# Two small additions to the leading products of ones in an attention-and-GLU kernel

## The chip, the core and the metric

The kernel runs on one core of one Trainium2 chip. The metric is the device time of one execution in microseconds (us); the figure given is the median of several runs. A profiled execution has a span, from its first to its last instruction, and a device time of its own, which is a little longer than the span.

## The reference

Two blocks follow each other. The first is a linear attention with a polynomial sketch: with batch 4, 4 heads, 1088 positions and head width 32, each q and k row is multiplied by S1 and S2 (8 x 32), and the outer product of the two results gives 64 features.

```
a = S1 @ x ;  b = S2 @ x ;  phi(x) = outer(a, b)          # 64 features
kv  = sum over s of phi(k)[f] * v[d]      z = sum over s of phi(k)[f]
num = phi(q) . kv                         den = phi(q) . z + 1e-6
attn = num / den                          # (batch, head, seq, 32)
x   = attn, heads side by side            # 4352 tokens x 128
out = (sigmoid(x @ w_gate) * (x @ w_val)) @ w_out        # d_ff = 1536
```

S1, S2 and the three weights reach the program as 64-bit floating-point numbers, seen as pairs of 32-bit words, and are narrowed to 32-bit floats on the chip. All products are of 32-bit floats; a product of a tile pair stands in the trace as two passes of TensorE.

## The kernel before, in words

**The steady part.** The tokens are cut into nine chunks of 512 (the last of 256), and d_ff into twelve blocks of 128. `w1` (L363) makes one "wave": x @ w_gate and x @ w_val for one chunk and one block, four passes of 512 columns. ScalarE takes the sigmoid (L371), VectorE multiplies (L384), and `w2` (L320, `moeout`) adds the product with w_out into a bank. `slot(group, waves)` puts a piece of attention work for the next batch between waves. This part runs from about 19 us to the end.

**The head.** Before the first wave, the attention of the first 512 tokens of batch 0 has to be made, in an order written out by hand; the engines run their own instruction streams in program order. Its steps are:

1. `warm(512, 512)` (call L265, products L261): products of a tile of ones by itself, whose results nobody reads. They need nothing but a memset, and so begin at 0.96 us. The tile they write is one of the two `wave` buffers.
2. S arrives by DMA and is narrowed (`narrow`: L97, L101, L105, L109, L117, L118, L127, on three engines). TensorE turns it (L803, `st`), and VectorE makes the masked copy `sk` (L813).
3. `kps` (L451): k times S for batch 0. VectorE transposes the result (L461, `kab`) and forms features of k in `outer` (L530), for the first five of nine blocks of positions.
4. `aps`, `bps` (L558): q times S, for two pairs of heads. ScalarE copies aps (L568); VectorE multiplies them to the features of q (L577, `qp`). In between stand `gram` (L474, L497), which gives the sum of k's features from small products, its copy (L483), and the mask (L508, L520), whose result `zb` is the denominator's weights.
5. `dps` (L730): the denominator. `kv0` (L638): the product of k's features and v, in two groups: the first five blocks, and the other four after VectorE has made their features. ScalarE copies the result (L674, `kvd`), TensorE turns it (L708, `ndps`), ScalarE copies that (L721, `nd`).
6. `nps` (L749): the numerator; VectorE divides it (L776) into `xT`, the input of the waves, in two halves of 256 tokens.
7. `warm(256)` (L261 again) between nps and the first wave. The first wave is cut into passes of 256 columns, so that it can begin with the first half of xT.

The first weights are narrowed in the same stretch: VectorE has their steps (L105, L109, L127) among those of the attention, POOL has L97 and L118, and ScalarE L101 and L117. All inputs come over the SP and ScalarE DMA queues, the last of the weights at about 23 us.

`warm` builds its operands from `ones` by access patterns that repeat one element:

```
def warm(*cols):
    t = psm.tile([P, 2, 512], F32, tag="wave", name="warm")
    one = [... [0, n] ... for n in cols]      # moving operand, n columns
    x = ... [0, P] ...                        # 128 x 128, stationary
    for r in one: nc.tensor.matmul(out=t[:, 0, :n], lhsT=x, rhs=r, ...)
```

## Time and profile before

| What | Value |
|---|---|
| five runs | 308.75, 309.13, 309.84, 312.97, 313.39 us |
| median | 309.84 us |
| profiled execution, device time | 308.75 us |
| profiled execution, span | 307.0 us |
| TensorE matmul rows busy | 299.2 us (97%) |
| VectorE / ScalarE / POOL busy | 155.3 / 80.8 / 34.4 us |
| waves, L363 | 436 passes, 191.8 us |
| moeout, L320 | 216 passes, 105.5 us |
| warm, L261 | 6 passes, 5.0 us |

A row of the timeline gives the start and the length in us, the engine, the line and operation, the tile written and those read, the shapes and a count; in brackets stands how long the engine had been idle before, and what ended that. Rows on TensorE overlap, since its passes are pipelined: how fast it works is seen from the distance between starts, or from the mean length of one pass of a given shape, and not from the busy share. PEld is its weight load, which can lie beside a pass.

### The profile page before, as it was taken

The page shows a single profiled execution, that of the slowest core. Times are in us where ns is not written, and L with a number is a line of the kernel's source. Part 1 is how long each engine was busy: PE and PEld are TensorE (multiplying, and loading weights), DVE is VectorE, ACT ScalarE, POOL GpSimd, SP SyncE. Part 2 cuts the span into 40 slices and gives each one's busy share as a digit, 9 for nine tenths or more (in the row PEclk, how much of TensorE's full clock was granted, in tenths as well). Part 3 has the DMA queues.
Part 4 walks back from the last instruction along what each step waited for, and adds up shares of the span by engine and source line. Part 5 has one row for each costly group of instructions (what it writes and reads, how often), then busy time and mean ns, then how long its engine had stood idle before and what let it go on. Part 6 is the DMA issues. An engine that isn't in the chain of part 4 may idle for free.

```text
span 307.0 us, 3600 instructions
## 1 busy us (share of the span) xinstructions
PE 299.2 (97%) x1360; PEld 138.2 (45%) x1360; DVE 155.3 (51%) x267; ACT 80.8 (26%) x150; POOL 34.4 (11%) x63
## 2 busy tenths in 40 slices
PE   7889999999999999999999999999999999999994
PEld 2544434444444444533444444444444444444683
DVE  6878889754736544463465542645232223222331
ACT  2356542322122222222123222212222222222220
POOL 1245551230000320000002300000000000000000
PEclk9999999999999999999999999999999999999999
DMA  7992422399402397242003960200001000200011
GB/s 223 320 343 53 124 59 117 81 194 180 153 0 34 78 161 109 61 108 91 0 0 81 184 118 2 35 0 2 0 12 22 0 0 5 31 0 0 7 28 17
DMA packets 29585, 23.29 MB, mean 76 GB/s; under 512 B 20928, under 2 KB 24512, under 8 KB 29568
## 3 DMA queue, kind: packets, MB, share of 16 engines
q1 hardware_dynamic: 25200, 15.21, 18.6%
q0 software_dynamic: 3456, 7.09, 13.4%
q10 hardware_dynamic: 912, 0.77, 0.9%
q8 instruction: 10, 0.16, 0.2%
q14 instruction: 7, 0.06, 0.1%
HBM read 19.80 MB, written 3.26 MB: 75 GB/s over the span
## 4 chain that ended last, share of the span: by engine, by line
PE 96%; DVE 1%; DMA 1%; issue 0%; ACT 0%; SPq 0%; DVEq 0%
PE wave L363 57%; PE moeout L320 30%; PE nps L749 2%; PE dps L730 2%; PE kvz L652 1%; PE kps L451 1%; DMA s_in<-in_S_dram 1%; PE kvz L638 1%; PE cqps L597 1%; PE gram L474 0%; PE bps L558 0%; PE warm L261 0%; PE ndps L708 0%; PE aps L558 0%; DVE kT L428 0%
## 5 line engine op out<-in xcount | busy, mean ns | idle before, releaser
L363 PE MATMUL wave<-xT,w_sb 128*128 128x512 f32 (+1 forms) x436 | 191.8, 566 | 0.0
L384 DVE TENSOR_TENSOR g<-wave,sg 128x512 f32<-128x512 f32 x102 | 70.3, 689 | 130.6 <-ACT sg L371 130.2
L363 PEld LDWEIGHTS wave<-xT,w_sb 128*128 128x128 f32 x436 | 83.2, 191 | 93.0 <-issue 88.5
L371 ACT ACTIVATE sg<-wave 128x512 f32<-128x512 f32 x102 | 60.9, 597 | 201.7 <-PE wave L363 201.7
L320 PE MATMUL moeout<-g,w_sb 128*128 128x512 f32 (+1 forms) x216 | 105.5, 576 | 0.0
L320 PEld LDWEIGHTS moeout<-g,w_sb 128*128 128x128 f32 x216 | 39.5, 190 | 43.6 <-issue 38.5
L621 POOL DMA_DIRECT2D qp<-dq x12 | 7.0, 588 | 110.3 <-DMA dq<-cq 110.3
L118 POOL TENSOR_TENSOR head<-head,tail 128x384 int32<-128x384 int32 (+2 forms) x14 | 13.4, 955 | 20.4 <-DVE head L109 14.2
L530 DVE TENSOR_TENSOR kp<-kab 128x1152 f32<-128x1152 f32 (+2 forms) x10 | 10.8, 1095 | 0.0
L630 DVE TENSOR_TENSOR qp<-qp,bq 128x1152 f32<-128x1152 f32 (+1 forms) x7 | 9.1, 1294 | 2.4 <-DMA bq<-dq 2.4
L109 DVE SCALAR_TENSOR_TENSOR head<-cap,head 128x384 int32<-128x384 int32 (+2 forms) x14 | 7.5, 535 | 0.5
L330 DVE STREAM_TRANSPOSE o_sb<-moeout 128x512 f32<-128x512 f32 (+1 forms) x9 | 6.1, 679 | 2.6 <-PE moeout L320 2.5
L730 PE MATMUL dps<-qp,zb 128*32 128x256 f32 (+1 forms) x64 | 5.8, 434 | 1.4 <-DVE zb L520 1.4
L621 POOL DMA_DIRECT2D bq<-dq x12 | 6.9, 576 | 0.5 <-DMA out_dram<-o_sb 0.2
L127 DVE SCALAR_TENSOR_TENSOR w_sb<-square,head 128x384 f32<-128x384 f32 (+1 forms) x11 | 5.7, 519 | 2.5 <-POOL head L118 2.1
L776 DVE TENSOR_TENSOR xT<-nps,rb 128x576 f32<-128x576 f32 (+2 forms) x9 | 5.9, 660 | 1.9 <-PE nps L749 1.3
L101 ACT ACTIVATE tail<-w_in 128x384 int32<-128x384 uint32 (+1 forms) x13 | 6.6, 522 | 0.9 <-DMA w_in<-in_moe_w_out_dram 0.9
L97 POOL TENSOR_SCALAR cap<-w_in 128x384 f32<-128x384 f32 (+1 forms) x13 | 6.5, 503 | 0.5 <-DMA w_in<-in_moe_w_out_dram 0.5
L749 PE MATMUL nps<-qp,nd 64*32 64x256 f32 (+1 forms) x128 | 6.0, 432 | 0.4 <-ACT nd L721 0.4
L765 DVE STREAM_TRANSPOSE rb<-rc 128x576 f32<-128x576 f32 (+2 forms) x9 | 6.1, 681 | 0.3
L261 PE MATMUL warm<-ones 128*128 128x512 f32 (+1 forms) x6 | 5.0, 972 | 1.0 <-DVE hm L267 1.0
L439 DVE STREAM_TRANSPOSE qT<-kq 128x512 f32<-128x512 f32 (+1 forms) x8 | 5.7, 714 | 0.0
(73 smaller groups left out, 86.9 us busy)
## 6 DMA issues: line engine op xcount, KB each, us to landing
qp<-dq POOLq DMA_DIRECT2D x12, 288.0 KB, 9.2
bq<-dq POOLq DMA_DIRECT2D x12, 288.0 KB, 9.4
v<-in_v_dram SPq DMA_DIRECT2D x16, 144.0 KB, 6.0
kq<-in_k_dram SPq DMA_DIRECT2D x3, 544.0 KB, 3.9
kq<-in_q_dram SPq DMA_DIRECT2D x3, 544.0 KB, 5.2
w_in<-in_moe_w_gate_dram SPq DMA_DIRECT2D x6, 256.0 KB, 5.8
w_in<-in_moe_w_val_dram SPq DMA_DIRECT2D x6, 256.0 KB, 5.5
w_in<-in_moe_w_out_dram SPq DMA_DIRECT2D x6, 256.0 KB, 6.9
```

Source lines behind the costliest of these rows:

```text
L101: nc.scalar.activation(out=tail, in_=lo, func=ACTF.Copy, scale=2.0**-29)
L109: nc.vector.scalar_tensor_tensor(out=head, in0=cap, scalar=-0x40000000, in1=head, op0=ALU.bitwise_and, op1=ALU.bitwise_or)
L118: nc.gpsimd.tensor_tensor(out=head, in0=head, in1=tail, op=ALU.add)
L320: nc.tensor.matmul(out=moe["acc"][:, :tw], lhsT=w_sb[:, 2, j, :], rhs=g[:, jj, :tw], start=(j == 0), stop=(j == NJ - 1),)
L363: nc.tensor.matmul(out=wv[:, which, jj * tw + o : jj * tw + o + tp], lhsT=w_sb[:, which, j0 + jj, :], rhs=xT[:, t0 + o : t0 + o + tp], sta ...
L371: nc.scalar.activation(out=sg, in_=wv[:, 0], func=ACTF.Sigmoid)
L384: nc.vector.tensor_tensor(out=g, in0=wv[:, 1], in1=sg, op=MUL)
L530: nc.vector.tensor_tensor(out=KP[b][:, pi, j0:j1].rearrange("p j m (i l) -> p (j m) i l", i=R), in0=bass.AP(tensor=a0.tensor, offset=a0.of ...
L621: get.dma_start(out=t[64 * c : 64 * c + 64, n * H * W1 : (n + 1) * H * W1], in_=bass.AP(tensor=d0.tensor, offset=d0.offset, ap=rows + [[1, ...
L630: nc.vector.tensor_tensor(out=q0, in0=q0, in1=half(BQ[b], n), op=MUL)
L730: nc.tensor.matmul(out=dps[32 * h : 32 * h + 32, :w], lhsT=zb[b % 2][:, h, :], rhs=half(QP[b], n)[:, 2 * (h % 2) + h // 2, :], start=True, ...
L749: nc.tensor.matmul(out=t[32 * h : 32 * h + 32, c, :w], lhsT=ND[b][rows, 32 * h : 32 * h + 32], rhs=half(QP[b], n)[rows, 2 * (h % 2) + h // ...
```

## The change

The first call of `warm` gets a third product, of 128 columns. A second call, of one product of 128 columns, stands after the turning of S (L803) and before everything that reads its result; on TensorE's stream it comes between `st` and `kps`. Each product is two passes with two weight loads. The second call takes a `wave` buffer of its own, so the later users of that pair of buffers change places. Line numbers after L807 rise by one. TensorE's stream of 398 listed rows has 400; the streams of the other engines hold the same instructions in the same order.

```
-    warm(512, 512)
+    warm(512, 512, 128)
...
     nc.tensor.matmul(out=st_[:, : 2 * R], lhsT=s4..., rhs=ident[...], is_transpose=True, ...)
+    warm(128)
     st_ = st_[:, : 2 * R].rearrange("p (n r) -> p n r", n=2)
     sk = const.tile([P, 2, 2, R], F32, tag="sk")
     nc.vector.tensor_tensor(out=sk, ...)
```

## The prediction

> **What bounds the kernel now.** I read the page first, then TensorE's groups by form in two stretches, then the timelines of TensorE and VectorE up to 20 us. The page shows TensorE on 96% of the chain that ended last.

> ```profile
> span 307.0 us, 3600 instructions
> PE 299.2 (97%) x1360; PEld 138.2 (45%) x1360; DVE 155.3 (51%) x267; ACT 80.8 (26%) x150; POOL 34.4 (11%) x63
> PEclk9999999999999999999999999999999999999999
> PE 96%; DVE 1%; DMA 1%; issue 0%; ACT 0%; SPq 0%; DVEq 0%
> ```

> From 30 us on TensorE stands idle for 3.9 of 277 us. Whatever the head gains or loses before the first wave therefore moves the end by as much, as long as the weights keep up. So the change is worth what it does to the first 23 us.

> The clock row claims full clock throughout, and it is misleading. The same shape takes two lengths. First TensorE's groups by form up to 19.3 us, then from 20 us; the last number before the second bar is the mean length of a pass in ns:

> ```profile
> L451 PE MATMUL kps<-kT,sk 64*32 64x288 f32 x16 | 1.2, 685 | 0.4 <-DVE sk L813 0.4
> L749 PE MATMUL nps<-qp,nd 64*32 64x256 f32 x16 | 1.1, 631 | 0.4 <-ACT nd L721 0.4
> L730 PE MATMUL dps<-qp,zb 128*32 128x256 f32 x8 | 1.1, 631 | 1.4 <-DVE zb L520 1.4
> L363 PE MATMUL wave<-xT,w_sb 128*128 128x256 f32 x1 | 0.6, 634 | 0.0
> L638 PE MATMUL kvz<-kp,v 128*32 128x64 f32 x64 | 2.2, 314 | 0.0
> ```

> ```profile
> L451 PE MATMUL kps<-kT,sk 64*32 64x288 f32 x48 | 2.1, 415 | 0.0
> L749 PE MATMUL nps<-qp,nd 64*32 64x256 f32 x48 | 2.0, 388 | 0.0
> L730 PE MATMUL dps<-qp,zb 128*32 128x256 f32 x24 | 1.9, 391 | 0.0
> L363 PE MATMUL wave<-xT,w_sb 128*128 128x256 f32 x53 | 12.4, 379 | 0.0
> L652 PE MATMUL kvz<-kp,v 128*32 128x64 f32 x192 | 3.3, 220 | 0.0
> ```

> The distances between starts say it plainly: 0.853 us from one 512-column pass of warm to the next, 0.429 in the later waves; 0.427 us for 256 columns at 18.97, 0.216 from 19.97 on. The pass between, from 19.40 to 19.75, took 0.350, so the clock doubled at about 19.67. **TensorE ran at half speed through the whole head**, although 3.41 us of products of ones stand in front of it.

> [...]

> **Part one: 128 more columns at the start.** 128 columns are a quarter of 0.853: 0.213 us a pass, 0.43 for the two, from 4.53 to 4.96; if each waits for its own weight load (0.34 us, the third and fourth of L261), to about 5.1. st waits for `s` until 5.09 and starts at 5.15. Cost at the end: 0 to 0.1 us, hidden by the wait for S. Should S come early, the cost is the whole 0.43.

> **Part two: 128 columns between st and kps.** The gap is in the timeline of TensorE:

> ```profile
> 0.96 3.78 PE L261 MATMUL warm<-ones 128*128 128x512 f32 x4 [0.96 <-DVE hm L267]
> 5.15 0.28 PE L803 MATMUL st<-ident,s 16*128 16x16 f32 x1 [0.41 <-DVE s L127]
> 5.84 1.22 PE L451 MATMUL kps<-kT,sk 64*32 64x288 f32 x16 [0.41 <-DVE sk L813]
> ```

> The nearest row for warm squeezed behind other work is warm(256): its weight load began 0.18 us after nps had streamed, its first pass 0.16 later, and the second weight load took 0.33. Two 128-column passes so placed need about 0.7 us from their first weight load, at 5.4, and let kps go at 6.1 instead of 5.845. Queued behind it are kps and, through it, kab and all of VectorE's head. I take +0.25 for both parts together; the ends are 0 (the passes just fill the gap) and 0.45.

> **What the two buy.** [...] The full clock then comes at 6.01, not 19.67. [...] The head at full speed, step by step:

> - kps starts at 6.1; its second round follows after 0.24, not 0.48, and a row is 0.415 long, not 0.685. kab, at 7.16 before, starts at 6.9.
> - VectorE's kab and kp take 2.29 us as before, to 9.19. Meanwhile aps (1.09 halved), gram (cannot start before kab's first half at 7.3; about 0.8 because of its 36 weight loads) and bps (1.2 halved) end by 8.9. So qp starts at 9.19 and no longer waits for bps. Gain 1.38.

> ```profile
> 7.16 0.85 DVE L461 STREAM_TRANSPOSE kab<-kps 128x288 f32<-128x288 f32 x2 [0.76 <-PE kps L451]
> 10.57 1.29 DVE L577 TENSOR_TENSOR qp<-bps,asb 128x512 f32<-128x512 f32 x2 [1.12 <-PE bps L558]
> 16.43 0.42 DVE L127 SCALAR_TENSOR_TENSOR w_sb<-square,head 128x256 f32<-128x256 f32 x1 [0.33 <-ACT square L117]
> 18.14 0.42 DVE L776 TENSOR_TENSOR xT<-nps,rb 128x256 f32<-128x256 f32 x1 [1.28 <-PE nps L749]
> ```

> - zb and the second half of kp keep that gain: kp ends at 12.06. dps (11.0) and the first group of kv0 end about then. The second group, 1.08 before, takes about 0.6, so kvd starts at 12.8 where it was 15.77. v landed by 9.4.
> - kvd to nps took 1.15; ndps is 0.2 shorter; nps starts at 13.8 and is done by 14.5.
> - VectorE, however, has dT, the reciprocal, rb and five narrowing steps: 13.44 to 16.86 before, 3.4 us with 0.4 of waits. It reaches xT at 15.3, not 18.14: **VectorE takes over the bound**, and the 1.28 us wait for nps goes. Gain 2.85.
> - warm(256) is over by then (it held the first wave from 18.56 to 18.97), and the first eight passes lose their 0.34 of half speed. But the first moeout needs `g` and a narrowed w_out block, which VectorE reached 4.33 us after the first xT; that stays about 4.2. So moeout goes from 22.95 to about 19.9. **Gain 3.0 us**, from there carried to the end.

> The DMAs allow it: w_out's first block landed at 11.2, those of the next pair at 14.0 where their narrowing, at 16.94 before, is wanted at about 14; the later ones have 4 us and more to spare. If that cover failed, the loss is 0.3. The exchanged wave buffers cost nothing: the program's waits on them are the same.

> The sum: 308.75 - 3.0 = 305.75 for a run like the profiled one, span 304.0. The median stands 1.09 above the profiled run. The lowest three runs average 309.24, half a microsecond above it, so I add 0.5: **306.2 us**, 1.2% under 309.84. A measurement of this kernel can tell about 1% from no change, that is 306.74 or less.

> **Rivals.**

> *The clock does not come earlier, or came early in other runs already (0.20).* [...] Against it: none of five runs lies below the late one profiled. Then only the products' +0.25 counts, or the gain is in both kernels: 309.0 to 310.1, say 309.5.

> *The clock comes, but VectorE and the narrowing eat the gain (0.12).* VectorE is over 90% busy from 19 to 26 us. If the weights' chain over three engines shifts by only half of what the attention gains, 1.5 us remain: 307.7. For it: moeout already waited for w_sb in before. Against: POOL and ScalarE have idle time there.

> *The clock comes early and is taken back (0.08), the slower one.* [...] Each us at half clock in the waves costs 0.5. A loss at 16.25 and a return at 19.67 cost 1.7 and leave a gain. The rival decides from a return later than about 22 us; a return at 30 us, (30 - 16.25) / 2 = 6.9 more than 306.2, gives 313.1, which is where the two highest runs of before lie.

> **How the numbers follow.** Forecast 0.60: its own range is 305.0 to 307.4 (kps' delay 0 to 0.45, gain 2.3 to 3.7); about 0.47 falls under 306.74. The rest of it, 0.13, with the first two rivals, 0.32, makes 0.45 within 1%. The slower rival gives 0.08. The range takes in the first rival: 304.9 to 310.2, leaving out the slower one and a few hundredths.

> **What would show it.** Right: the groups by form up to 15 us show kps near 415 ns, dps near 390, kvz near 220; kps starts near 6.1; xT near 15.3; the first wave near 15.7; moeout near 19.9. Part two is wrong if kps starts after 6.4. The forecast falls if kps and nps still take 685 and 631 ns, or if wave passes of 0.853 us appear after 16 us.

## The result and the profile after

The change made no difference that can be measured: the ratio of its executions to those of the kernel before is 0.9983, with a 95% interval of 0.9964 to 1.0002. Medians were 307.57 us (43 executions) and 308.88 us (80). The profiled execution of the changed kernel has a span of 305.7 us and a time of 307.46 us. The comparison leaves out executions more than 1.5% above a kernel's fastest; where I count spans below, I take all but those over 370 us, because the spread itself turned out to be the subject.

First the page of the changed kernel: span, busy times, clock row, chain.

```profile
span 305.7 us, 3608 instructions
PE 298.3 (98%) x1364; PEld 138.5 (45%) x1364; DVE 155.3 (51%) x267; ACT 80.7 (26%) x150; POOL 34.7 (11%) x63
...
PEclk9879999999999999999999999999999999999999
...
PE 96%; DVE 1%; DMA 1%; issue 1%; ACT 0%; SPq 0%; DVEq 0%
```

TensorE is 96% of the chain, as before. The clock row has a dent in its second and third slice, between 7.6 and 22.9 us, where the row of before had none. TensorE's groups by form show what it is. First from 5.6 to 12.3 us, then from 12.4 to 19.1 us:

```profile
L451 PE MATMUL kps<-kT,sk 64*32 64x288 f32 x16 | 0.7, 415 | 0.0
L638 PE MATMUL kvz<-kp,v 128*32 128x64 f32 x32 | 0.7, 221 | 0.2 <-issue 0.2
L730 PE MATMUL dps<-qp,zb 128*32 128x256 f32 x8 | 0.6, 387 | 1.2 <-DVE zb L520 1.2
```

```profile
L363 PE MATMUL wave<-xT,w_sb 128*128 128x256 f32 x6 | 2.6, 614 | 0.0
L749 PE MATMUL nps<-qp,nd 64*32 64x256 f32 x16 | 1.1, 630 | 0.4 <-ACT nd L721 0.4
L638 PE MATMUL kvz<-kp,v 128*32 128x64 f32 x32 | 1.1, 314 | 0.0
```

kps, dps and half of kvz run at full speed (415, 387, 221 ns). The other half of the same kvz takes 314, and nps and the first wave stand where they stood before. **The clock came early, and was taken back in the middle of kv0.** The trace's clock records say when: full speed from 5.53, half from 12.36, full from 19.19 us. The distances between those are 6.83 us each, twice the 3.41 that lie between two changes in the profile of e1_first below (10.85 and 14.26). The view of five stretches of that length, the changes on their edges (columns: stretch, its length, busy us and rows of each engine, granted clock, DMA) shows the stretch before the loss:

```profile
core 0: us, PE busy (x) PEld busy (x) DVE busy (x) ACT busy (x) POOL busy (x), PEclk, DMA share, GB/s
...
5.53:8.95 3.42, 3.32 (x86) 1.63 (x86) 3.16 (x7) 1.52 (x5) 0.54 (x2) 1.00 1.06 239
8.95:12.36 3.41, 1.81 (x50) 1.16 (x50) 3.38 (x9) 1.21 (x4) 1.36 (x4) 1.00 1.08 296
12.36:15.77 3.41, 2.67 (x57) 1.25 (x49) 2.35 (x7) 2.06 (x7) 1.90 (x4) 0.50 1.06 371
15.77:19.19 3.42, 3.42 (x16) 2.74 (x9) 3.14 (x8) 0.69 (x2) 1.29 (x3) 0.50 1.07 375
```

From 8.95 to 12.36 VectorE is busy for 3.38 of 3.41 us and TensorE for 1.81. TensorE waits for VectorE there, 1.18 us of it for zb before dps, and at the end of that stretch the clock is gone. The next two stretches have PEclk 0.50; in the second TensorE is busy for all of its 3.42 us, and at its end the clock is back.

So of the forecast 3.0 us, what is left in this execution is 307.0 - 305.7 = 1.3. The timeline of TensorE in it, and below it three rows of the kernel before:

```profile
5.45 0.51 PE L261 MATMUL warm<-ones 128*128 128x128 f32 x2
5.93 0.72 PE L451 MATMUL kps<-kT,sk 64*32 64x288 f32 x16
...
10.79 0.64 PE L730 MATMUL dps<-qp,zb 128*32 128x256 f32 x8 [1.18 <-DVE zb L520]
...
16.79 4.80 PE L363 MATMUL wave<-xT,w_sb 128*128 128x256 f32 x12
21.61 1.13 PE L320 MATMUL moeout<-g,w_sb 128*128 128x512 f32 x2
```

```profile
12.39 1.08 PE L730 MATMUL dps<-qp,zb 128*32 128x256 f32 x8 [1.36 <-DVE zb L520]
...
18.97 3.95 PE L363 MATMUL wave<-xT,w_sb 128*128 128x256 f32 x12
22.95 1.12 PE L320 MATMUL moeout<-g,w_sb 128*128 128x512 f32 x2
```

dps is 1.6 us earlier than before, the first wave 2.2, moeout 1.3: the waves start early and then run at half speed until 19.19, one of the signs that the prediction had named for its forecast to fall.

### The profile page after: what moved, and what is told of

Read it like the earlier page. It is cut to its first block, busy times and chain, and to the rows that moved or that the text cites. A ratio compares the mean times of both kernels' runs of the same rounds, so it can differ in the third digit from the quotient of the medians.

```text
span 305.7 us, 3608 instructions
## 1 busy us (share of the span) xinstructions
PE 298.3 (98%) x1364; PEld 138.5 (45%) x1364; DVE 155.3 (51%) x267; ACT 80.7 (26%) x150; POOL 34.7 (11%) x63
## 4 chain that ended last, share of the span: by engine, by line
PE 96%; DVE 1%; DMA 1%; issue 1%; ACT 0%; SPq 0%; DVEq 0%
PE wave L363 58%; PE moeout L320 30%; PE nps L749 2%; PE dps L730 2%; PE kvz L652 1%; PE kps L451 1%; DMA s_in<-in_S_dram 1%; PE cqps L597 1%; PE kvz L638 1%; PE warm L261 1%; PE ndps L708 0%; PE gram L474 0%; PE kvz L661 0%; DVE qp L577 0%; PE bps L558 0%
## 5 line engine op out<-in xcount | busy, mean ns | idle before, releaser
L363 PE MATMUL wave<-xT,w_sb 128*128 128x512 f32 (+1 forms) x436 | 192.6, 568 | 0.0
L363 PEld LDWEIGHTS wave<-xT,w_sb 128*128 128x128 f32 x436 | 83.8, 192 | 93.3 <-issue 88.7
L630 DVE TENSOR_TENSOR qp<-qp,bq 128x1152 f32<-128x1152 f32 (+1 forms) x7 | 9.1, 1294 | 1.7 <-DMA bq<-dq 1.7
L261 PE MATMUL warm<-ones 128*128 128x512 f32 (+2 forms) x10 | 5.9, 735 | 1.0 <-DVE hm L267 1.0
L776 DVE TENSOR_TENSOR xT<-nps,rb 128x576 f32<-128x576 f32 (+2 forms) x9 | 5.9, 660 | 1.8 <-PE nps L749 1.1
L127 DVE SCALAR_TENSOR_TENSOR w_sb<-square,head 128x384 f32<-128x384 f32 (+1 forms) x11 | 5.6, 518 | 1.7 <-POOL head L118 1.6
L730 PE MATMUL dps<-qp,zb 128*32 128x256 f32 (+1 forms) x64 | 5.3, 404 | 1.2 <-DVE zb L520 1.2
L749 PE MATMUL nps<-qp,nd 64*32 64x256 f32 (+1 forms) x128 | 6.0, 432 | 0.4 <-ACT nd L721 0.4
```

Of the source, the lines that this page charges most:

```text
L261: nc.tensor.matmul(out=t[:, 0, :n], lhsT=x, rhs=r, start=True, stop=True)
L363: nc.tensor.matmul(out=wv[:, which, jj * tw + o : jj * tw + o + tp], lhsT=w_sb[:, which, j0 + jj, :], rhs=xT[:, t0 + o : t0 + o + tp], sta ...
L630: nc.vector.tensor_tensor(out=q0, in0=q0, in1=half(BQ[b], n), op=MUL)
L730: nc.tensor.matmul(out=dps[32 * h : 32 * h + 32, :w], lhsT=zb[b % 2][:, h, :], rhs=half(QP[b], n)[:, 2 * (h % 2) + h // 2, :], start=True, ...
L749: nc.tensor.matmul(out=t[32 * h : 32 * h + 32, c, :w], lhsT=ND[b][rows, 32 * h : 32 * h + 32], rhs=half(QP[b], n)[rows, 2 * (h % 2) + h // ...
```

## The experiments

Two theories stood at first. **W**: the clock's windows lie at random against the start of an execution; the kernel before gets the clock early in about half of its executions too, and the change gets it more often but often loses it in the stretch from 9 to 15 us. **V**: the early clock comes and stays, and VectorE and the narrowing eat what it gives. A "window" is a stretch of 3.413 us like those in the view above: all changes of the clock inside a profiled execution lie one or more such stretches apart (3.41, 6.83 and 13.65 us early in the runs, 286.72 us, 84 times 3.413, in the profile of before).

A way to count serves all of the runs. The mean granted clock of an execution knows nothing of the time before the first grant (0.999 in the profile of before, at half speed until 19.67), but half a window's worth is missing in it for each window at half speed after that (0.989 in the profile of after, with 6.83 us of it). One such window in 305 us gives 0.994, two 0.989, four 0.978. I call an execution "withdrawn" if its mean is under 0.9955. The others kept an early clock or got it late, and the mean can't tell which; a span near 304 speaks for an early one, and one of 306 or more mostly for a late one. By that, the kernel before withdrew in 30 of 68, 18 of 45, 17 of 36 and 4 of 11 executions in the four comparisons below; of the first 68, just one has the span of a kept early clock (304.0 us). The change withdrew in 22 of 43, and 10 of the 21 others have spans up to 304.6. So by this count the clock came early in 31 of 68 executions before and in 32 of 43 of the change, and of these 32 it was lost in 22.

### The parts alone, none, and the pause filled

Four kernels on one chip.

No leading products:

```
-    warm(512, 512)
```

> No leading products of ones at all; the 256 columns before the first wave stay. Theory W (the clock's windows lie at random against the start; the kernel before is granted early in about half of its executions, and the change is granted early but often loses it again in the thin stretch from 9 to 15 us): without the products no execution is granted before about 16 us, so the spans lose their low end: none under 306, median about 308.5, ratio to before about 1.002 to 1.005, and no execution shows a withdrawn clock (mean clock 0.997 or more in all). Theory V (the early clock comes but VectorE and the narrowing eat its gain): spread and median like before, ratio 0.999 to 1.001.

Ratio 1.0039 (1.0017 to 1.0061). No span is under 306.4; 3 of 22 executions were withdrawn, all with spans over 311 us. I had expected no withdrawal at all; these three may have lost the clock elsewhere than in the head (no withdrawn execution among the 68 has a span over 308.1). The leading 512 and 512 are worth 0.4%, and the low end of the kernel before is theirs. Its profile gets the clock at 20.04 us.

First part alone:

```
-    warm(512, 512)
+    warm(512, 512, 128)
```

> Only the third product of 128 columns at the start. Theory W: the leading run of products is 0.4 us longer, so some more executions are granted early (by 0.43 / 3.41, about one in eight), each worth 1 to 3 us less the withdrawals: ratio 0.998 to 1.000. Theory V: no difference, 1.000.

Ratio 0.9985 (0.9960 to 1.0010). 14 of 22 executions were withdrawn against 30 of 68 of the kernel before, a difference that so few executions do not establish. Its profile is one: granted at 4.02, taken at 10.85, given again at 14.26, span 304.5.

Second part alone:

```
     # after the turning of S
+    warm(128)
```

> Only the 128 columns between st and kps. Theory W: the gap closed there fills the windows that begin between 2 and 3.4 us, which 512 and 512 alone do not fill; most of the change's early grants come from this one, and it costs kps 0.1 to 0.25 us: ratio 0.998 to 1.001. Theory V: its cost alone, 1.0005 to 1.001.

Ratio 1.0012 (0.9991 to 1.0034). Half were withdrawn (11 of 22). That most of the change's early grants come from this part, as I had expected, does not show: counted as above, 12 of 22 executions were early here and 15 of 22 with the first part alone. By chance its profile shows the case that the prediction had worked out, a clock granted at 4.85 and kept. TensorE's timeline, with VectorE's row for xT after it:

```profile
5.98 0.72 PE L451 MATMUL kps<-kT,sk 64*32 64x288 f32 x16
...
10.83 0.64 PE L730 MATMUL dps<-qp,zb 128*32 128x256 f32 x8 [1.18 <-DVE zb L520]
...
15.08 3.71 PE L363 MATMUL wave<-xT,w_sb 128*128 128x256 f32 x12
19.14 1.13 PE L320 MATMUL moeout<-g,w_sb 128*128 128x512 f32 x2 [0.35 <-DVE w_sb L127]
```

```profile
14.28 0.42 DVE L127 SCALAR_TENSOR_TENSOR w_sb<-square,head 128x256 f32<-128x256 f32 x1
14.61 0.41 DVE L776 TENSOR_TENSOR xT<-nps,rb 128x256 f32<-128x256 f32 x1
```

kps at 5.98, xT at 14.61 with no wait for nps, moeout at 19.14 waiting for the narrowed weights, span 304.0 us. That speaks against V: where the clock stays, VectorE does become the bound, and 3.0 us of gain remain.

The change, with the pause before dps filled:

```
     spread_z()
+    warm(512, 512)
```

> The change, and two passes-pairs of 512 columns of ones behind the spreading product of gram (L497), where TensorE waits about 1.3 us for zb. Theory W: the window there streams 60% and not 37%, so far fewer executions lose the clock; mean clock under 0.995 in at most a quarter of them (18 of 43 in the change), spans near 304 in most, ratio to before 0.992 to 0.995. Theory V: no gain, 0.998 to 1.001. If the products delay dps when the clock is at half speed, up to 0.4 us are lost there.

Ratio 0.9925 (0.9899 to 0.9951), median 305.8 us. No execution of 15 was withdrawn, and 11 have spans of 303.7 to 304.4. Its timeline and its stretches between edges:

```profile
6.29 0.72 PE L451 MATMUL kps<-kT,sk 64*32 64x288 f32 x16 [0.21 <-DVE sk L814]
...
9.55 0.41 PE L497 MATMUL gram<-gh,e_sum 128*128 128x32 f32 x2 [0.34 <-POOL gh L485]
9.80 1.97 PE L261 MATMUL warm<-ones 128*128 128x512 f32 x4
11.70 0.64 PE L730 MATMUL dps<-qp,zb 128*32 128x256 f32 x8
```

```profile
4.05:7.46 3.41, 2.45 (x38) 1.07 (x36) 3.01 (x9) 0.64 (x4) 0.45 (x2) 1.00 1.02 306
7.46:10.87 3.41, 3.07 (x67) 1.78 (x58) 3.38 (x8) 1.84 (x5) 1.29 (x3) 1.00 1.09 258
10.87:14.28 3.41, 3.02 (x84) 1.60 (x82) 3.34 (x9) 1.31 (x4) 1.40 (x2) 1.00 1.06 375
```

TensorE is busy for 3.07 and 3.02 us in the two stretches that cover the pause, and the clock is 1.00 throughout. This settles it between W and V, for W.

The filling is not free. Its products take 1.97 us where the pause in e2_second was 1.18, and dps follows kps by 5.41 us here and by 4.85 there, moeout by 13.69 and 13.16. So about half a us of the gain is paid for holding it. A shorter filling was not run.

### Which part holds, once the pause is filled

Four kernels on another chip. The kernel before, with the same filling:

```
     warm(512, 512)
...
     spread_z()
+    warm(512, 512)
```

> The kernel before with the same products of ones in the pause behind gram, and without the change. Theory W: the pause's products keep the early clock of the executions that have it (30 of 68 runs of the kernel before showed it withdrawn); the others stay late: about half of the spans near 304, half at 306.4 to 308, no withdrawn clock; ratio 0.995 to 0.998. If the pause's products alone were what helps, it would come to the 0.9925 of the change with them.

Ratio 0.9966 (0.9940 to 0.9992). Withdrawals fell to 5 of 22, and only five executions have spans of 303.7 to 304.0. I had expected about half of the spans near 304 and no withdrawal. So the filling alone does not give the 0.9925. Its profile was withdrawn at another place, the gaps around st that the second part of the change would fill:

```profile
5.33 0.23 PE L803 MATMUL st<-ident,s 16*128 16x16 f32 x1 [0.81 <-DVE s L127]
6.03 0.72 PE L451 MATMUL kps<-kT,sk 64*32 64x288 f32 x16 [0.47 <-DVE sk L813]
```

```profile
4.17:7.58 3.41, 2.13 (x39) 0.73 (x38) 3.11 (x9) 0.68 (x4) 0.46 (x2) 1.00 1.01 258
7.58:10.99 3.41, 3.41 (x55) 2.03 (x54) 2.74 (x5) 1.82 (x5) 1.03 (x3) 0.50 1.09 227
```

Granted at 4.17, TensorE then waited 0.81 us for s and 0.47 for sk, and at 7.58 the clock was gone again. The filling then ran at half speed (3.76 us, 1.97 in e4_hold) and held dps back to 13.78 us. The next run shows that the first part can do without the second here: its profile has the same two waits (0.78 and 0.47 us) and keeps the clock.

First part with the filling, without the second (against e4_hold):

```
     # after the turning of S
-    warm(128)
```

> The first part of the change (128 more columns at the start) and the pause's products, without the 128 columns behind st. Theory W: between the kernel before with the pause's products and the whole change with them: 0.993 to 0.996, some more late executions than with the second part.

Ratio 0.9918 (0.9892 to 0.9943), no withdrawal in 17. The second part adds nothing that shows beside the first, if the pause is filled. My expectation, a value between the two neighbours, fell. Seven of the 17 spans lie above 304.6 us, against two of 11 in e6_hold2 on the same chip; that is too few to tell.

Whole change, pause filled, and one more filling behind kv0:

```
         narrow_01(0, 2)
+        warm(256)
         ndt(0)
```

> The change, the pause's products, and 256 columns of ones behind kv0, in the second pause (0.5 us before ndps). Theory W: with the first pause filled no window falls under a third any more, so the second filling adds nothing: 0.991 to 0.994, same as without it; if the products meet a half-speed clock they delay ndps by 0.2 us.

Ratio 0.9917 (0.9885 to 0.9948), one withdrawal in 11, as expected no difference.

A third leading product of 256 columns, pause filled (against e4_hold):

```
-    warm(512, 512, 128)
+    warm(512, 512, 256)
```

> The change with a third leading product of 256 columns and not 128, and the pause's products. Theory W: when S comes late, or the edges lie unluckily, the longer lead still fills a window; fewer late executions than the 4 of 15 over 305 with 128: 0.990 to 0.993. Against: in an execution not yet granted at 4.5 us the products last until 5.4 us and delay st by 0.2 us.

Ratio 0.9906 (0.9872 to 0.9939) in 6 executions, five of them 303.7 to 304.3. Better than 128 columns it can't be called, the intervals overlap. Its profile got the clock only at 7.18 and shows the price of the products at half speed: the two passes of 128 columns before kps took 0.80 us (0.51 in the profile of after), and kps started at 6.47 us, where sk had been ready at 6.04.

### The tail that withdrawals do not explain

Four of 15 executions of e4_hold were not withdrawn and still took 305.1 to 306.8 us. Some of these may have got the clock late, as the profile of e8_hold256 did (7.18 us, span 305.5). But the profile of e7_first_hold has an early clock (full speed from 3.96) and a span of 306.4, with these waits on TensorE after 19 us (columns: engine and line, what it waited for, us in total, times, longest):

```profile
PE moeout L320 <- DVE g L384: 1.2, 1, 1.2
PE dps L730 <- DVE qp L630: 0.8, 1, 0.8
PE moeout L320 <- DVE w_sb L127: 0.6, 1, 0.6
```

L630 multiplies q features that went to DRAM and back. An earlier head asks for them earlier: theory **D**. The test is one wave more between sending and product, for the first batch alone. It ran on another chip than e4_hold, which was repeated beside it:

> The change with the pause's products once more, on another chip, with the shifted kernels beside it. Theory W: 0.991 to 0.995 again, no withdrawn clock in the executions; most spans 303.7 to 304.4, and a tail up to 307 that the clock does not explain.

0.9896 (0.9853 to 0.9939) in 5 executions, spans 303.6 to 304.6.

```
-    slot(q01, 6)
+    slot(q01, 7)
...
-    slot(lambda: part(0, 1, lambda: narrow_w(NJ - 1, 3)), 2)
+    slot(lambda: part(0, 1, lambda: narrow_w(NJ - 1, 3)), 1)
```

> As e4_again, and one wave more (7, not 6) between the sending of the first q features through DRAM and their product (L630), with one less behind. Theory D (the tail comes from that transfer, which in the profile with 306.4 us made dps wait 0.8 us for L630, since an earlier head asks for it earlier): the low spans stay at 303.7 to 304, the tail gets shorter, ratio 0.0005 to 0.002 under e4_again. If the tail comes from another transfer (the one for batch 1) or from S, no difference to e4_again.

0.9946 (0.9925 to 0.9966): slower than expected. The shift brought a wait that I had not seen. The last weight block is narrowed inside part(0, 1), and the twelfth wave now came right behind it:

```profile
47.56 1.96 PE L363 MATMUL wave<-xT,w_sb 128*128 128x512 f32 x4 [1.39 <-DVE w_sb L127]
```

Every span is up by about that, to 305.2 and more; but 14 of 15 lie within 0.8 us.

> The kernel before with the same shift of one wave alone. Theory W: the shift without the clock is worth little: 0.998 to 1.000.

The same shift on the kernel before: 1.0059 (1.0030 to 1.0088), against the expectation. Its profile has the same wait of 1.39 us. It also shows the kernel before's head with an early clock that is lost: granted at 4.65, taken at 8.06 after kps had waited 1.10 us for sk, and back only at 21.71, span 309.5.

The last step of the narrowing in front of part(0, 1), against e9_hold_later:

```
+    narrow_w(NJ - 1, 3)
-    slot(lambda: part(0, 1, lambda: narrow_w(NJ - 1, 3)), 1)
+    slot(lambda: part(0, 1), 1)
```

> As e9_hold_later, but the last step of the last weight block's narrowing stands before part(0, 1) and not inside its division, so that the twelfth wave needn't wait the 1.4 us for w_sb that the shift brought. Theory D (the tail of the held executions, up to 3 us over 303.7, comes mainly from the first q features' trip through DRAM): spans 303.7 to 304.5 in nearly all, ratio 0.989 to 0.992. If the tail has other causes, it is as long as without the shift (4 of 15 over 305), ratio about 0.9925.

0.9903 (0.9866 to 0.9940), 6 executions on a third chip, all 304.0 to 304.4. The tail did not show, which is what D says; but six executions, and a tail of 4 in 20 without the shift (e4_hold and e4_again together), don't prove it.

The profile of e7_first_hold itself gives D's first batch only the smaller part. Here are two of its uses of L630, and TensorE's longest wait, which follows the second:

```profile
40.26 2.17 DVE L630 TENSOR_TENSOR qp<-qp,bq 128x1152 f32<-128x1152 f32 x1 [0.21 <-DMA bq<-dq]
76.19 1.36 DVE L630 TENSOR_TENSOR qp<-qp,bq 128x1152 f32<-128x1152 f32 x1 [4.58 <-DMA bq<-dq]
78.20 1.13 PE L320 MATMUL moeout<-g,w_sb 128*128 128x512 f32 x2 [1.22 <-DVE g L384]
```

The 0.8 us of dps belong to the first batch: the features came 0.21 us late, and L630 then took 2.17 us instead of the 1.35 of every other profile. The 1.2 us of moeout stand behind the second batch's features, for which VectorE waited 4.58 us, and the shift doesn't touch these. So what made the tail stays open.

## Why the prediction was wrong

**The reading of the clock was right for the execution that was read.** TensorE did run at half speed in its head (a pass of kps took 685 ns, 415 from 20 us on), the profile of the change had the full clock early, and the steps up to dps came out: kps at 5.93 (6.1), kab at 6.75 (6.9), qp at 8.96 (9.19), dps at 10.79 (11.0). No run shows the 6.01 us at which the forecast lets the full clock come, an estimate of the author: it came at 5.53 in the profile of the change, at 4.02 in that of e1_first and at 4.85 in that of e2_second.

**The gain was about right where the clock stays.** In the profile of e2_second, xT was at 14.61 (forecast 15.3), moeout at 19.14 (19.9), span 304.0 (304.0). That the span fits to a tenth is partly luck: moeout came 3.8 us earlier than before, not 3.0, and 0.8 was lost again behind it, 0.46 of that in one wait for g at 75.79. e4_hold, where no execution was withdrawn, has 0.9925, and its commonest span is 303.7 to 304.1, with the filling's half us in it.

**The cost was too high.** +0.25 us for kps: in the changed kernel kps starts 0.05 us after sk is ready (5.74 + 0.14), as before. The clock was granted at 5.53 there, and the squeezed products, 0.51 us from 5.45 on, fit the gap. At half speed, and with the longer lead, e8_hold256 shows 0.43.

**What failed are two steps that turned one execution into a median.**

1. "None of five runs lies below the late one profiled" was taken as evidence that the kernel before is always late. It isn't: 40 to 47% of its executions in the three larger comparisons were withdrawn, and the profiles of e5_before_hold and e10_before_later show its head with an early clock that is lost. I priced this at 0.20 and took the late profile as the standing case. The five runs were a poor sample, by chance or by their chip: of the 75 executions that were added later, 36 lie below the 308.75 us that none of the first five undercut. And a span does not always tell a withdrawn execution from a late one: of the 30 in the first comparison, 21 lie at 304.7 to 305.9 us, but nine at 306.0 to 308.1, where the late ones are.
2. The early clock was assumed to stay. The third rival, 0.08, named the loss, and a price: 1.7 us for a loss at 16.25 and a return at 19.67. No run shows a loss at 16.25, from which the 313.1 is counted as well; in the trace of the change the clock was gone from 12.36 to 19.19, right after the window from 8.95 to 12.36. I looked in that rival only for a way to be slower, and left out of the forecast its commonest form, in which it merely takes back about half the gain. It came in 22 of 43 executions. The window that lost the clock was not idle: TensorE was busy for 1.81 us of it. In the profile the loss came 3.9 us earlier than I priced and lasted 6.83 us, not 3.4; that it cost 305.7 - 304.0 = 1.7 all the same is a coincidence. The gain works against itself here: before, TensorE waits 1.36 us of the 6.55 between the starts of kps and dps, after it 1.52 of 4.86 (0.34 for gram, 1.18 for dps), a larger share of a shorter stretch.

Together: nearly half of the executions of before already had part of the gain (their median span is 305.4, that of the others 307.25), and half of those after kept only part of it (median 305.8; 305.7 in the profiled one, 1.3 of the 3.0). The 3.0 us of the sum became 0.17%. This is an account and not a closed sum: 11 further executions of the change have spans of 305.0 to 309.4 without a withdrawal, and which of them were late is not known.

One thing stays open: whether the 0.17% is a gain at all. The interval holds 1, and neither part alone differs from 1.

## What to carry to other kernels

Here TensorE ran its head at half speed in some executions, and in others got the full clock early and lost it again. That is worth two questions: does something earn the full clock, and does everything after that keep it? Products of ones in front answered only the first (32 of 43 executions early, 22 of them lost it); a filling in the longest pause in which TensorE waits for VectorE answered the second (lost in none of 15), and brought the ratio from 0.9983 to 0.9925. And one profile is one position of the windows, whose first edge lay at 0.61 to 2.97 us in five profiles: read the mean clock and the span of many executions before taking its stretches for the typical ones.
